# Windowed attention with two mixtures of experts: attention blocks folded on GpSimd before their transposes, the attention loop re-staggered

## The chip, the cores and the metric

The kernel runs on one core of a Trainium2 chip. The core has five engines that run their own instruction streams in order and meet through semaphores: TensorE (PE in the profile, with its weight loads as PEld), VectorE (DVE), ScalarE (ACT), GpSimd (POOL) and SyncE (SP, which here only issues DMAs). The metric is the device time of one execution in microseconds, the median of several runs.

## The reference

Three stages follow one another. Only the first is touched by the change.

```python
# q, k, v: [4 batches, 8 heads, 576 positions, 64]
scores = q @ k.T / 8 + slopes[head] * -|i - j|
scores = where(0 <= i - j < 128, scores, -1e9)        # a causal window of 128
attn = exp(scores - max(scores))
attn = attn / (sum(attn) + 1e-9)
x = (attn @ v)  -> [2304 tokens, 512]
# stage 2: soft mixture of experts
logits = x @ phi;  d = softmax over tokens;  c = softmax over slots
slots = d.T @ x;   slots = relu(slots @ w1[e]) @ w2[e];  x = c @ slots
# stage 3
out = relu(x @ w_in) ** 2 @ w_out
```

## The kernel before

**Tiling.** Heads are taken in pairs, so a unit `u` is one of 16 (batch, head pair) combinations. Its 576 queries are cut into nine chunks `c` of 64; the 64 queries of both heads fill the 128 partitions. Because of the window, a chunk sees at most three blocks of 64 keys: its own (the causal triangle), the one before (whole) and the one before that (the opposite triangle). So a score tile is 128x192, narrower for chunks 0 and 1. For a given query the triangle of the first block and that of the last one don't overlap: where one holds a weight, the other holds an exact zero.

**The attention loop.** Two consecutive chunks are one step `t`, and 72 steps cover all units. In loop iteration `t` these are written out, in this order, with manual scheduling (each engine executes its instructions in the order in which they are written):

- `emit_S(t + 1)`: two score matmuls into one of three PSUM banks "S".
- `emit_T(t - 3)`: transposes of the finished weights `p` through TensorE, into two of three PSUM banks "T": `tp` holds the blocks that fill 128 rows ("full"), `tq` those of which half is used ("half").
- `emit_PV(u)`, once in four or five steps: 24 matmuls of the transposed weights `ptb` with `v`.
- `emit_evac(t - 3, 0)`: ScalarE copies `tp` into `ptb`.
- `emit_max(t)`: VectorE adds the bias table and takes the row maximum, two instructions.
- `emit_add(t - 1)`: VectorE adds 1e-9 to the sums.
- `emit_exp(t)`: ScalarE, two exponentials with their row sums.
- `emit_norm(t - 1)`: VectorE takes reciprocals, GpSimd multiplies `p` by them, two instructions of 128x192.
- `emit_evac(t - 3, 1)`: VectorE copies the halves in `tq` into `ptb`, up to two instructions.
- `run_side(t)`: what belongs to a whole unit (`emit_xT`: ScalarE evacuates the PV result and `load_v` follows; `emit_xn`: four transposes of it and a VectorE copy), and once a batch, the logits (`emit_logits`, `emit_logr`) and the online softmax over tokens (`emit_d0` to `emit_d4`).

The loads of the next units' `z` (queries) and `k`, and one or two weight tiles of 1 MB for the second stage, are issued on SP's queue just after the score matmuls of a unit's last chunk. They land in a unit's buffers (two of each), so they wait until those score matmuls have read them. Five `p` buffers go round. `ptb` is a ring of seven groups of four 128x128 blocks; a unit takes five of them.

**After the loop** come the rest of the last batch's softmax and logits, the expert matmuls (`H`, `O`), whose weights are read while attention runs and after it, and the last stage with its 864 `acc` matmuls. Five weight tiles can only be loaded when the pools of the attention close (`load_extra`).

Of the kernel before, what the change touches and what calls it, by code (L numbers as in the profile page):

```python
# [24 lines left out]
LT = 3  # L25
# [3 lines left out]
def attn_moe_relu2_kernel(ctx: ExitStack, tc: tile.TileContext, z, k, v, phi, w1, w2, w_in, w_out, bias, cst, out):  # L29
# [22 lines left out]
    ef = const.tile([128, 32], F32, name="ef")  # L52
# [99 lines left out]
    for g in range(2 * NS):  # L152
        u, c = divmod(g, NCH)
        n = 64 * min(3, c + 1)
        e = 192 if c % 2 or (c == 0 and g % 2) else 0
        info.append((u, c, n, e))
# [11 lines left out]
    def emit_max(t):  # L168
        for i in range(2):
# [5 lines left out]
                scale=-0.125, scalar=3.0e38, op0=ALU.add, op1=ALU.min, accum_out=st_t[t][:, i:i + 1],  # L175
# [3 lines left out]
    def emit_exp(t):  # L179
        st = st_t[t]  # L180
        for i in range(2):
            u, c, n, e = info[2 * t + i]
            p = pbuf[t % NP][:, e:e + n]
            act.activation(out=p, in_=p, func=AF.Exp, bias=st[:, i:i + 1], scale=-1.0, accum_out=st[:, 2 + i:3 + i])  # L184

    def emit_add(t):
        st = st_t[t]
        dve.tensor_scalar(out=st[:, 2:4], in0=st[:, 2:4], scalar1=1e-9, scalar2=None, op0=ALU.add)  # L188

    def emit_norm(t):  # L190
        st = st_t.pop(t)
        dve.reciprocal(out=st[:, 4:6], in_=st[:, 2:4])
        for i in range(2):
            u, c, n, e = info[2 * t + i]
            p = pbuf[t % NP][:, e:e + n]
            eng = dve if t >= NS - 2 and i == 1 else pool
            eng.tensor_scalar(out=p, in0=p, scalar1=st[:, 4 + i:5 + i], scalar2=0.0, op0=ALU.mult, op1=ALU.add)  # L197

    def emit_T(t):
        full, half, P = [], [], pbuf[t % NP]
        for u, c, n, e in info[2 * t:2 * t + 2]:
            if c % 2:
                full.append((jblk(u, c // 2) + 1, e + n - 128))
                if n == 192:
                    half.append((64, jblk(u, c // 2 - 1) + 3, e))
            else:
                half.append((0, jblk(u, c // 2), e + n - 64))
                if n == 192:  # L210
                    full.append((jblk(u, c // 2 - 1) + 2, e))
        full.sort(key=lambda x: x[0])
        A = bank("T", "tp")[:, 0:256].rearrange("p (a b) -> p a b", a=2)
        B = bank("T", "tq")[:, 0:256].rearrange("p (a b) -> p a b", a=2)
        for i, (slot, e) in enumerate(full):
            pe.transpose(A[:, i, :], P[:, e:e + 128], ident)  # L216
        if len(half) == 2 and half[0][0] != half[1][0]:
            pe.transpose(B[:, 0, :], P[:, 128:256], ident)  # L218
            dst = [(ptb[r:r + 64, slot], B[r:r + 64, 0]) for r, slot, e in half]
        else:  # L220
            dst = []
            for i, (r, slot, e) in enumerate(half):
                assert r == 0 and e <= 256
                pe.transpose(B[:, i, :], P[:, e:e + 128], ident)  # L224
                dst.append((ptb[0:64, slot], B[0:64, i]))
# [150 lines left out]
    dve.memset(ptb[64:128, 0::4], 0.0)  # L376
    dve.memset(ptb[0:64, 3::4], 0.0)
# [682 lines left out]
```

## Time and profile before

| | |
|---|---|
| median of 3 runs | 402.41 us (402.33 to 402.83) |
| span of the profiled execution (first to last instruction) | 400.7 us |
| left around the span, by the median | 1.7 us |
| attention, first score matmul to the end of the last PV | 3.6 to about 130 us |
| PE / DVE / ACT / POOL busy over the span | 97 / 74 / 61 / 23 % |

The page gives busy times for the whole span, in which the last stage (from about 170 us, TensorE alone) weighs most. For the attention loop one reads stretches of it: the busy time of each engine between two points, the chain of work that ended last (followed back from the last instruction, at each step to what released it), and the rows of single forms of instructions. A PE row's duration includes the pipeline behind it, so the cost of one more matmul is read from the distance between starts, which is what the chain's pieces show.

### The profile page before, as it was taken

What the parts mean: (1) busy time and instruction counts of PE and PEld (TensorE: products, weight loads), DVE (VectorE), ACT (ScalarE), POOL (GpSimd) and SP (SyncE); (2) the same over time, 40 slices, a digit from 0 to 9 for tenths busy, and PEclk for the clock granted to TensorE, in tenths of its full rate; (3) what the DMA queues carried; (4) which work ended last, traced back from release to release, by engine and by line L of the source; (5) the groups of instructions that cost most, each with busy time, mean ns of one, the idle gap of its engine ahead of it and who ended that gap; (6) DMA issues with size and microseconds to landing.
All of it is one profiled execution on the core that took longest, in us unless ns stands there. A gap on an engine that the chain in (4) does not pass through costs nothing.

```text
span 400.7 us, 7955 instructions
## 1 busy us (share of the span) xinstructions
PE 390.5 (97%) x2666; PEld 308.0 (77%) x2666; DVE 295.5 (74%) x967; ACT 244.4 (61%) x730; POOL 90.7 (23%) x188
## 2 busy tenths in 40 slices
PE   8899999999999999999999999999999999999995
PEld 8788878878876534687787888788877888888884
DVE  6798887779877685577867789786867775566454
ACT  5788878868876411178867765777657544433440
POOL 3445435335444041213111111211010000000000
PEclk9999999999999999999999999999999999999999
DMA  7969989869896999999602200000000040013004
GB/s 234 384 231 332 369 300 361 324 236 413 308 381 228 406 421 421 407 409 408 252 2 95 90 27 0 0 2 1 0 2 2 2 157 0 2 40 117 2 0 159
DMA packets 20489, 75.36 MB, mean 188 GB/s; under 512 B 2528, under 2 KB 4320, under 8 KB 16352
## 3 DMA queue, kind: packets, MB, share of 16 engines
q1 hardware_dynamic: 19872, 74.30, 48.4%
q10 hardware_dynamic: 576, 0.56, 0.5%
q8 instruction: 21, 0.34, 0.3%
q14 instruction: 20, 0.16, 0.1%
HBM read 70.13 MB, written 4.72 MB: 187 GB/s over the span
## 4 chain that ended last, share of the span: by engine, by line
PE 89%; DVE 6%; ACT 2%; DMA 1%; issue 1%; POOL 0%; DVEq 0%; POOLq 0%
PE acc L863 48%; PE s L165 9%; PE xa L250 6%; PE h L819 4%; PE H L627 4%; PE O L766 4%; PE tp L216 3%; DVE ptb L240 2%; DVE p L173 2%; PE tq L218 1%; PE X L291 1%; PE L L278 1%; PE MX L715 1%; DVE psum L881 1%; PE tq L224 1%; PE xb L250 1%
## 5 line engine op out<-in xcount | busy, mean ns | idle before, releaser
L863 PE MATMUL acc<-whl,arena_gh 128*128 128x512 f32 x864 | 216.4, 393 | 0.0
L863 PEld LDWEIGHTS acc<-whl,arena_gh 128*128 128x128 f32 x864 | 160.2, 188 | 35.2 <-issue 2.9
L848 DVE TENSOR_TENSOR arena_gh<-hT,arena_gh 128x384 fp32r<-128x384 f32 (+1 forms) x97 | 53.7, 553 | 29.5 <-ACT arena_gh L844 24.0
L197 POOL TENSOR_SCALAR p<-p,st 128x192 f32<-128x192 f32 (+1 forms) x142 | 56.2, 408 | 68.4 <-DVE ptb L240 28.1
L184 ACT ACTIVATE p<-p,st 128x192 f32<-128x192 f32 (+1 forms) x144 | 61.3, 428 | 11.2 <-DVE st L173 10.6
L831 ACT ACTIVATE acc<-h 128x384 f32<-128x384 f32 x47 | 23.1, 491 | 64.8 <-PE h L819 64.8
L165 PE MATMUL s<-kt,zq 128*128 128x192 f32 (+2 forms) x270 | 54.3, 326 | 0.1
L675 POOL TENSOR_SCALAR yw<-f 128x512 f32<-128x512 f32 x32 | 27.2, 852 | 100.6 <-DVE arena_cin L692 49.1
L240 DVE COPY ptb<-tq 64x128 f32<-64x128 f32 x128 | 35.3, 281 | 15.2 <-PE tq L218 13.9
L173 DVE CUSTOM_DVE_ANT_0 p<-s,tbl 128x192 f32<-128x192 f32 (+1 forms) x144 | 41.7, 325 | 2.4 <-PE s L165 1.9
L165 PEld LDWEIGHTS s<-kt,zq 128*128 128x128 f32 x270 | 41.7, 195 | 1.6 <-DMA kt<-in_k_dram 0.3
L238 ACT ACTIVATE ptb<-tp 128x256 f32<-128x256 f32 (+1 forms) x72 | 25.0, 348 | 13.1 <-PE tp L216 12.5
L819 PE MATMUL h<-cst_sb,Mst 128*128 128x384 f32 x95 | 32.2, 339 | 0.1
L250 PE MATMUL xa<-ptb,vt 128*64 128x256 f32 (+1 forms) x256 | 27.8, 359 | 0.0
L184 ACT ACTIVATION_READ_ACCUMULATOR p<-p,st 128x1 f32 x144 | 27.3, 189 | 0.0
L840 DVE TENSOR_TENSOR hT<-acc 128x384 f32<-128x384 f32 x17 | 9.5, 557 | 23.6 <-ACT acc L831 23.6
L216 PE MATMUL tp<-cs,p 128*128 128x128 f32 x128 | 26.5, 276 | 0.2 <-DVE st L188 0.2
L844 ACT ACTIVATE arena_gh<-hT 128x384 fp32r<-128x384 f32 x48 | 24.8, 516 | 0.6
L844 ACT ACTIVATE arena_gh<-acc 128x384 fp32r<-128x384 f32 x47 | 24.2, 515 | 0.6
L250 PEld LDWEIGHTS xa<-ptb,vt 128*64 128x64 f32 x256 | 17.0, 136 | 9.4 <-issue 1.8
L690 DVE SCALAR_TENSOR_TENSOR yw<-f,yw 128x512 int32<-128x512 int32 x32 | 22.4, 704 | 0.8
L831 ACT ACTIVATE hT<-h 128x384 f32<-128x384 f32 x48 | 22.7, 472 | 0.0
(206 smaller groups left out, 469.1 us busy)
## 6 DMA issues: line engine op xcount, KB each, us to landing
w_w<-in_w_dram SPq DMA_DIRECT2D x31, 1024.0 KB, 8.9
f<-in_w_in_dram SPq DMA_DIRECT2D x16, 512.0 KB, 10.6
f<-in_w_out_dram SPq DMA_DIRECT2D x16, 512.0 KB, 10.2
zq<-in_z_dram SPq DMA_DIRECT2D x13, 576.0 KB, 4.7
vt<-in_v_dram SPq DMA_DIRECT2D x16, 320.0 KB, 6.7
kt<-in_k_dram SPq DMA_DIRECT2D x13, 288.0 KB, 5.3
out_dram<-psum SPq DMA_DIRECT2D x11, 256.0 KB, 2.1
yw<-in_w_dram SPq DMA_DIRECT2D x1, 1024.0 KB, 11.9
```

The source lines that it names most:

```text
L165: pe.matmul(out=sb_t[t][:, 256 * i:256 * i + n], lhsT=zbuf(u)[:, c].rearrange("p a b -> p (a b)"), rhs=kt_t[u][:, 64 * c + 64 - n:64 * c + ...
L173: dve.tensor_tensor_reduce(out=p, in0=sb_t[t][:, 256 * i:256 * i + n], in1=tbl[:, 192 * pr + 192 - n:192 * pr + 192], scale=-0.125, scalar ...
L184: act.activation(out=p, in_=p, func=AF.Exp, bias=st[:, i:i + 1], scale=-1.0, accum_out=st[:, 2 + i:3 + i])
L197: eng.tensor_scalar(out=p, in0=p, scalar1=st[:, 4 + i:5 + i], scalar2=0.0, op0=ALU.mult, op1=ALU.add)
L216: pe.transpose(A[:, i, :], P[:, e:e + 128], ident)
L240: dve.tensor_copy(out=dst, in_=src)
L250: pe.matmul(out=out, lhsT=v_t[u][:, j, po:po + 64], rhs=pt[:, a:b, po:po + 64], start=(j == 0 or (j == 3 and a == 2)), stop=(j == 4 or (j ...
L819: pe.matmul(out=hb[-1][:, 0:HB], lhsT=Mst[:, 128 * f:128 * f + 128], rhs=cst_sb[:, c0:c0 + HB], start=True, stop=True)
L831: act.activation(out=rbuf[hf][:, cl], in_=hb[hf][:, cl], func=AF.Relu)
L844: act.activation(out=lo_t[i][1][hf][:, 0, cl], in_=rbuf[hf][:, cl], func=AF.Square)
L848: eng.tensor_tensor(out=gh[hf][:, 1, cl], in0=g[hf][:, cl], in1=gh[hf][:, 0, cl].bitcast(F32), op=ALU.subtract)
L863: pe.matmul(out=acc_t[s], lhsT=gh[:, x, c0:c0 + 128], rhs=w[:, f % 2, y, :], start=(units[i] in firsts and a == 0), stop=(units[i] in last ...
```

## The change

A block of scores that is three key blocks wide was transposed as one full 128-column piece and one piece of which a half was used. Now GpSimd first subtracts the far triangle block from the near one (`emit_fold`), so that a chunk's weights stand in 128 columns, the far ones with a minus sign. One transpose per chunk is left. When the transposed block is copied out, ScalarE's Relu keeps the positive part, and VectorE takes the part with the minus sign as max(-x, 0) for the other half.

Beside it: 1e-9 is added to the row sums on GpSimd for two steps at once, and one VectorE reciprocal serves two steps (`emit_sums`, `emit_recip`); the normalising multiplication covers 128 columns in place of 192; scores are computed two steps ahead; a step's transposes come four steps after it, and their evacuation five; PV, its evacuation and the batch work move accordingly; `p` has six buffers; `ptb` has six groups of four blocks and two single ones (a unit takes four and one); the small tile `ef` lies in `phi_sb`. The first two and last two steps keep shorter distances and single sums.

```diff
-LT = 3
+LT = 4
...
-    NP = 5
+    NP = 6
...
-    NBL = 7
-    ptb = apool.tile([128, 4 * NBL, 128], F32, name="ptb")
+    NBL = 6
+    ptb = apool.tile([128, 4 * NBL + 2, 128], F32, name="ptb")
...
-    def emit_add(t):
-        st = st_t[t]
-        dve.tensor_scalar(out=st[:, 2:4], in0=st[:, 2:4], scalar1=1e-9, scalar2=None, op0=ALU.add)
+    def emit_sums(t, n=2):
+        k = 2 * (t % 2)
+        st = st_t[t // 2]
+        pool.tensor_scalar(out=st[:, 4 + k:4 + k + 2 * n], in0=st[:, 4 + k:4 + k + 2 * n], scalar1=1e-9, scalar2=1.0, op0=ALU.add, op1=ALU.mult)
+
+    def emit_recip(t, n=2):
...
+        dve.reciprocal(out=st[:, 8 + k:8 + k + 2 * n], in_=st[:, 4 + k:4 + k + 2 * n])
+
+    def emit_fold(t):
+        both = [x for x in info[2 * t:2 * t + 2] if x[2] == 192]
...
+        pool.tensor_tensor(out=ap(True), in0=ap(True), in1=ap(False), op=ALU.subtract)
 
     def emit_norm(t):
-        st = st_t.pop(t)
-        dve.reciprocal(out=st[:, 4:6], in_=st[:, 2:4])
+        st, k = st_t[t // 2], 8 + 2 * (t % 2)
+        emit_fold(t)
         for i in range(2):
             u, c, n, e = info[2 * t + i]
-            p = pbuf[t % NP][:, e:e + n]
+            o = e + n - 128 if c % 2 else e
+            p = pbuf[t % NP][:, o:o + min(n, 128)]
...
-        for dst, src in tp_t[t][i]:
-            if i == 0:
-                act.activation(out=dst, in_=src, func=AF.Copy)
+        if i == 0:
+            dst, src = tp_t[t][0]
+            act.activation(out=dst, in_=src, func=AF.Relu)
+            return
+        for dst, src, neg in tp_t.pop(t)[1]:
+            if neg:
+                dve.tensor_scalar(out=dst, in0=src, scalar1=-1.0, scalar2=0.0, op0=ALU.mult, op1=ALU.max)
             else:
                 dve.tensor_copy(out=dst, in_=src)
...
+    alone = (0, 1, NS - 2, NS - 1)
+    T_at, sums_at = {}, {}
+    for t in range(NS):
+        T_at.setdefault(t + (LT - 1 if t in alone else LT), []).append(t)
...
+    E_at = {}
+    for t in range(NS):
+        E_at.setdefault(t + (LT if t < 2 else LT + 1 if t < NS - 2 else LT - 1), []).append(t)
```

**How it moves the instructions.** On TensorE, from one PV to the next, in the middle of the attention (`s` scores, `tp`/`tq` transposes, `xa`/`xb` PV, `X` the transposes of `emit_xn`), before:

```order
L250 MATMUL xa<-ptb,vt 64x256 x6
L250 MATMUL xa<-ptb,vt 64x128 x2
L250 MATMUL xb<-ptb,vt 64x64 x4
L165 MATMUL s<-kt,zq_94 128x192 x2
L216 MATMUL tp<-cs,p_96 128x128 x2
L218 MATMUL tq<-cs,p_96 128x128
L165 MATMUL s<-kt,zq_94 128x192 x2
L216 MATMUL tp<-cs,p_97 128x128 x2
L218 MATMUL tq<-cs,p_97 128x128
```

and now:

```order
L261 MATMUL xa<-ptb,vt 64x256 x6
L261 MATMUL xa<-ptb,vt 64x128 x2
L261 MATMUL xb<-ptb,vt 64x64 x4
L166 MATMUL s<-kt,zq_93 128x192
L166 MATMUL s<-kt,zq_92 128x64
L233 MATMUL tp<-cs,p_99 128x128 x2
L166 MATMUL s<-kt,zq_92 128x128
L166 MATMUL s<-kt,zq_92 128x192
L233 MATMUL tp<-cs,p_100 128x128 x2
```

A step's third transpose (`tq`) is gone and everything else of a step stands; over the program the transposes into the "T" banks of this loop are 144 in place of 208 (128 into `tp`, 80 into `tq`).

On GpSimd, two steps before (each line is one head pair's chunk):

```order
L197 TENSOR_SCALAR p_97<-p_97,st 128x192 [waits DVE_49,PE_49,Activation_49]
L197 TENSOR_SCALAR p_97<-p_97,st 128x192 [waits Activation_49]
L197 TENSOR_SCALAR p_98<-p_98,st 128x192 [waits DVE_49,PE_49,Activation_49]
L197 TENSOR_SCALAR p_98<-p_98,st 128x192 [waits Activation_49]
```

and two steps now, the sums first, then fold, norm, norm for either step:

```order
L190 TENSOR_SCALAR st<-st 128x4 [waits Activation_49]
L209 TENSOR_TENSOR p_95<-p_95 128x2x64 [waits PE_49]
L219 TENSOR_SCALAR p_95<-p_95,st 128x128 [waits DVE_49,Pool_49]
L219 TENSOR_SCALAR p_95<-p_95,st 128x128
L209 TENSOR_TENSOR p_96<-p_96 128x2x64 [waits PE_49]
L219 TENSOR_SCALAR p_96<-p_96,st 128x128 [waits Pool_49]
L219 TENSOR_SCALAR p_96<-p_96,st 128x128
```

Four instructions became seven; the first of them waits for ScalarE's exponentials of the later step, and VectorE's reciprocal waits for it.

On TensorE at the end of the loop, before (from the last score matmuls on):

```order
L165 MATMUL s<-kt,zq_93 128x192 x2
L216 MATMUL tp<-cs,p_98 128x128
L224 MATMUL tq<-cs,p_98 128x128 x2
L216 MATMUL tp<-cs,p_99 128x128 x2
L224 MATMUL tq<-cs,p_99 128x128
L250 MATMUL xa<-ptb,vt 64x256 x6
```

and now:

```order
L166 MATMUL s<-kt,zq_92 128x192 x2
L233 MATMUL tp<-cs,p_100 128x128 x2
L233 MATMUL tp<-cs,p_95 128x128 x2
L233 MATMUL tp<-cs,p_96 128x128 x2
L302 MATMUL X<-cs,xT_103 128x128 x4
L306 MATMUL Y<-cs,xT_103 128x128
L233 MATMUL tp<-cs,p_97 128x128 x2
L233 MATMUL tp<-cs,p_98 128x128 x2
L233 MATMUL tp<-cs,p_99 128x128 x2
L261 MATMUL xa<-ptb,vt 64x256 x6
```

The scores of the last step come before more of the remaining transposes, and the last PV but one comes later. The last batch's first logits (`L`), which stood ahead of the last PV, now stand behind it.

## Rows read from the trace of the kernel before

**Rows 1.** Busy time by stretch: us, engine busy (x instructions), clock, DMA share, GB/s.

```profile
15.70:122.00 106.30, 104.73 (x989) 87.70 (x989) 88.16 (x507) 85.12 (x359) 48.23 (x123) 1.00 0.87 331
122.00:128.46 6.46, 5.74 (x71) 3.90 (x68) 5.43 (x26) 4.08 (x17) 3.45 (x8) 1.00 0.62 226
```

**Rows 2.** Chain of waits, 15.7 to 122 us, its shares by line.

```profile
by line: PE s L165 29.5%; PE xa L250 21.9%; PE tp L216 9.1%; DVE ptb L240 6.0%; PE X L291 4.5%; DVE p L173 4.3%; PE tq L218 4.1%; PE tq L224 3.4%; PE xb L250 3.0%; PE R L336 2.9%; PE L L278 2.9%; issue 1.5%; DVE st L192 1.3%; PE L L284 1.2%
```

**Rows 3.** Chain of waits, 15.7 to 43 us: start us, us, what.

```profile
15.75 1.66 PE xa L250 x16
...
18.82 0.65 PE s L165 x4
19.47 0.22 PE tp L216 x2
19.69 0.11 PE tq L218
...
29.30 1.67 PE xa L250 x16
```

**Rows 4.** Chain of waits, 43 to 62 us, where it leaves TensorE.

```profile
47.51 0.29 DVE ptb L240
...
47.82 0.28 DVE ptb L240
48.10 0.27 DVE p L173
...
48.66 0.09 DVE st L188
...
48.77 0.17 DVE st L192
...
48.97 0.29 DVE ptb L240
```

**Rows 5.** Groups by form, 22 to 118 us: count, busy us, mean ns, idle before.

```profile
L184 ACT ACTIVATE p<-p,st 128x192 f32<-128x192 f32 x87 | 38.7, 446 | 7.7 <-DVE st L173 7.3
L240 DVE COPY ptb<-tq 64x128 f32<-64x128 f32 x99 | 27.4, 281 | 11.4 <-PE tq L218 10.5
L238 ACT ACTIVATE ptb<-tp 128x256 f32<-128x256 f32 x42 | 15.7, 373 | 6.5 <-PE tp L216 6.0
L296 DVE COPY xn_all<-X 128x512 f32<-128x512 f32 x13 | 8.9, 683 | 0.2
L262 ACT ACTIVATE xT<-xa 128x512 f32<-128x512 f32 x13 | 7.5, 581 | 1.1 <-PE xa L250 1.1
```

**Rows 6.** GpSimd's groups by form, whole span.

```profile
L197 POOL TENSOR_SCALAR p<-p,st 128x128 f32<-128x128 f32 x16 | 6.0, 372 | 5.6 <-DVE st L192 2.1 <-PE s L165 1.4 <-ACT p L184 1.4
L197 POOL TENSOR_SCALAR p<-p,st 128x64 f32<-128x64 f32 x16 | 5.1, 317 | 14.8 <-PE s L165 5.5 <-ACT p L184 5.1 <-DVE st L192 4.2
L707 POOL TENSOR_TENSOR whl<-arena_co,whl 128x512 fp32r<-128x512 f32 x2 | 2.6, 1278 | 10.6 <-ACT whl L706 10.6
L935 POOL COPY stat<-arena_gh 128x1 f32<-128x1 f32 x1 | 0.2, 183 | 8.8 <-DVE arena_gh L848 8.8
```

**Rows 7.** Instructions in order of time, end of the attention loop.

```profile
123.33 1.74 PE L250 MATMUL xa<-ptb,vt 128*64 128x256 f32 x16
...
124.58 0.34 DVE L173 CUSTOM_DVE_ANT_0 p<-s,tbl 128x192 f32<-128x192 f32 x1
...
126.86 0.86 PE L278 MATMUL L<-xT,phi_sb 128*32 128x128 f32 x24
...
128.46 1.74 PE L250 MATMUL xa<-ptb,vt 128*64 128x256 f32 x16
...
130.24 0.60 ACT L262 ACTIVATE xT<-xa 128x512 f32<-128x512 f32 x1 [1.33 <-PE xa L250]
```

**Rows 8.** Loads of `k`: from issue to landing.

```profile
DMA to landing us min/median/max: 2.8/5.2/7.5
```

More of the change, by code (lines that the diff above doesn't have):

```diff
@@ L154, in attn_moe_relu2_kernel @@
         n = 64 * min(3, c + 1)
-        e = 192 if c % 2 or (c == 0 and g % 2) else 0
+        e = 192 + 192 - n if c % 2 else 192 if c == 0 and g % 2 else 0
         info.append((u, c, n, e))
@@ new lines, in emit_recip, with ap @@
+    def emit_recip(t, n=2):
+        k = 2 * (t % 2)
+        st = st_t[t // 2]
+        dve.reciprocal(out=st[:, 8 + k:8 + k + 2 * n], in_=st[:, 4 + k:4 + k + 2 * n])
+    def emit_fold(t):
+        both = [x for x in info[2 * t:2 * t + 2] if x[2] == 192]
+        both.sort(key=lambda x: x[3])
+        if not both:
+            return
+        def ap(near):
+            o = [e + (0 if near == (c % 2 == 0) else 128) for u, c, n, e in both]
+            x = pbuf[t % NP][:, o[0]:o[0] + 64]
+            l = [list(y) for y in x.ap]
+            return bass.AP(tensor=x.tensor, offset=x.offset, ap=[l[0], [o[-1] - o[0], 2], [1, 64]]) if len(o) == 2 else x
+        pool.tensor_tensor(out=ap(True), in0=ap(True), in1=ap(False), op=ALU.subtract)
@@ L201, in emit_T @@
     def emit_T(t):
-        full, half, P = [], [], pbuf[t % NP]
+        full, rest, P = [], [], pbuf[t % NP]
         for u, c, n, e in info[2 * t:2 * t + 2]:
[L204 to L207, printed above, removed]
-            else:
-                half.append((0, jblk(u, c // 2), e + n - 64))
-                if n == 192:
-                    full.append((jblk(u, c // 2 - 1) + 2, e))
+            if c == 0:
+                rest.append((e, 0, jblk(u, 0), False))
+            elif c % 2:
+                full.append((jblk(u, c // 2) + 1, e + n - 128, (64, jblk(u, c // 2 - 1) + 3, True) if c > 1 else None))
+            else:
+                full.append((jblk(u, c // 2 - 1) + 2, e, (0, jblk(u, c // 2), True)))
@@ L212, in emit_T @@
         full.sort(key=lambda x: x[0])
         A = bank("T", "tp")[:, 0:256].rearrange("p (a b) -> p a b", a=2)
[L214 to L225, printed above, removed]
+        for i, o in enumerate([x[1] for x in full] + [x[0] for x in rest]):
+            pe.transpose(A[:, i, :], P[:, o:o + 128], ident)
@@ L226, in emit_T @@
         sl = [x[0] for x in full]
         st = sl[1] - sl[0] if len(sl) == 2 else 1
-        if st < 0:
-            raise AssertionError
-        tp_t[t] = [(ptb[:, sl[0]:sl[-1] + 1:st], A[:, 0:len(sl)])], dst
+        half = [(i, *x[2]) for i, x in enumerate(full) if x[2]] + [(len(full) + i, *x[1:]) for i, x in enumerate(rest)]
+        tp_t[t] = (ptb[:, sl[0]:sl[-1] + 1:st], A[:, 0:len(sl)]), [(ptb[r:r + 64, slot], A[r:r + 64, i], neg) for i, r, slot, neg in half]
     def jblk(u, j):
-        return 4 * ((5 * u + j) % NBL)
+        return 4 * ((4 * u + j) % NBL) if j < 4 else 4 * NBL + u % 2
```

63 lines of the change are left out of this document (37 added, 26 removed).

## The prediction

> **What bounds the kernel now.** I read three views of the attention loop, which ends near 130 us; the change touches nothing behind it. First the busy times of its even part, 15.7 to 122 us: TensorE is busy for 104.7 of 106.3 us, VectorE and ScalarE for 83 and 80%, GpSimd for 45% [rows 1]. A busy TensorE may be a pipeline that is only long, so the chain of waits comes second. Its shares by line add up to some 83% on TensorE (scores 29.5%, PV 25%, `tp` and `tq` 16.6%) and to 12% on VectorE [rows 2]. Third, the chain piece by piece, which has two patterns. From 15.75 to 29.30 us, two units, it never leaves TensorE (but for 0.02 us): four score matmuls in 0.65 us, two `tp` in 0.22, one `tq` in 0.11, and the next scores start at once [rows 3]. Elsewhere it runs through VectorE step after step: two half copies of 0.29 and 0.28, two maxima of 0.27, the addition 0.09, the reciprocal 0.17, and 1.46 us after the first copy the next step's copy [rows 4].
>
> So two engines are nearly level. Two units cost TensorE 13.55 us where it never waits [rows 3]. Between the PV at 15.75 and the one at 123.33 lie 14 units [rows 3, 7], 15.37 us a pair. The batch work on the chain (lines 278, 284, 336: 7.0% of 106.3 us, 7.4 us [rows 1, 2]) is 1.06 a pair. TensorE thus needs 14.6 of 15.37 us, and what it waits is at most 0.76 a pair, 5.3 us in all. VectorE has nine steps of 1.46, less two halves that a pair of units lacks (0.56), and two `xn` copies of 0.683 [rows 4, 5]: 13.9 us before batch work, the same as TensorE.
>
> One rule of the Trainium skill (Perfetto Trace Analysis, Identifying the Most-Contended Engine) says to judge TensorE's headroom by the share of its weight loads, not of its matmuls. That row says 87.7 of 106.3 us, 82% [rows 1], a level with VectorE. By that rule TensorE would have a sixth of its time free here; it is a rival below. A chain that stays on TensorE through two whole units speaks against it.
>
> **What the change takes from TensorE.** 144 transposes are left of 208. Each stands in the chain with 0.11 us [rows 3], in stretches without a wait as in the others: 64 x 0.11 = 7.0 us, eight per pair of units, and 13.55 becomes 12.67. Nothing else of a step's TensorE work changes. If another engine set the pace everywhere, this would be worth nothing; 7.0 is the upper end unless waits go too.
>
> **VectorE.** The addition goes (0.09 and 0.02 to its next), and every second reciprocal (0.17 and 0.03) [rows 4]: 9 x 0.11 + 4.5 x 0.20 = 1.9 us a pair, 13.9 becomes 12.0. The 112 halves that are now max(-x, 0) read the same 64x128 from PSUM as the copies, 281 ns [rows 5]; I take them at that price. Off the path, a tenth more would cost 112 x 0.03 = 3.4 us of an engine that has 12% room.
>
> **ScalarE.** The count stays; Relu replaces Copy in 72 evacuations at 373 ns [rows 5]. Nine steps of two exponentials (446 ns) and one evacuation are 11.4 us, two `xT` 1.2 [rows 5]: 12.5 us a pair, an upper figure because neighbours overlap.
>
> **GpSimd.** This is where the work goes. Its normalisations shrink: a 128x128 one takes 372 ns, a 128x64 one 317 [rows 6]; 16 and two a pair are 6.6 us. The fold is not in the trace of before. It reads two blocks and writes one, at most 128 columns, so it is bounded below by the 128x128 row with one input (372 ns) and above by the only two-input row, 1278 ns for 512 columns [rows 6]. The 64 and 128 rows give a fixed part of 262 ns and 0.86 ns a column; with that fixed part the 512 row gives 1.98 ns a column for two inputs, so an estimate of 0.52 us for two blocks and 0.39 for one. It is nearer to the upper row in kind and to the lower one in size, and I take 0.52. A pair of units has six of the one and two of the other: 3.9 us. The sums lie between the 183 ns of one column and the 317 of 64 [rows 6]; 4.5 x 0.25 = 1.1. GpSimd then needs 11.6 us a pair, after 7.0 now (45% of 15.37 [rows 1]).
>
> With batch work TensorE needs 12.67 + 1.06 = 13.7 us a pair; the other three 11.6 to 12.5 before theirs. TensorE stays first, by about a tenth, so its saving is not handed to another engine at once.
>
> **The new wait.** A reciprocal now waits for GpSimd's sums, they wait for both steps' exponentials, and they are queued behind the multiplications of the two steps before. Behind the reciprocal on VectorE stand that step's halves and the next maxima, and ScalarE waits for those. What hides it: scores lie two steps ahead in place of one, transposes come a step later, and two transposes need one "T" bank where three needed two, so TensorE may run a step further from the others. Before, a `tq` waited for the previous evacuation, and 11.4 us of VectorE's idle time before its copies are waits for `tq` [rows 5]. I can't price cover gained against latency added. So I leave TensorE's waits as they are: 0, with bounds of -3 (more than half of the 5.3 go) and +4 (they nearly double).
>
> **The ends.** At the start scores and loads come in the same pieces; 0, within 0.5 either way. At the end, before, the last maximum ends at 124.92 and the last PV starts at 128.46 [rows 7]. Now nine halves stand behind VectorE's last multiplication in place of six, 3 x 0.28 = 0.8 us; the last transposes no longer stand behind 1.1 us of logits (126.86 to 127.98); those logits follow the PV, where 0.6 us of `xT` hides half of them [rows 7]. Together between -0.6 and +1.4, and I take +0.5. What follows attention moves with it: the late weight tiles are issued when attention's pools close.
>
> **DMA.** 331 GB/s at a share of 0.87 [rows 1] are 35.2 MB, or 92 us at a full share. The stretch becomes about 99.5 us, so the loads fit, without much room. `k` lands 5.2 us after issue, 7.5 at worst [rows 8]; it is due about five steps later, 7.0 us at TensorE's own pace (5 x 12.67 / 9).
>
> **Sum.** 400.7 - 7.0 + 0.5 = 394.2 us of span; with the 1.7 us around it 395.9 against the median of 402.4.
>
> **The rivals.**
> - *The waits go as well.* With a bank to spare and scores further ahead the chain never leaves TensorE, as in [rows 3]: another 3 us, 392.9. For it: the first 28 us have no wait already, and VectorE loses 1.9 us a pair. Against: the batch stretches give every engine a burst that no buffer covers.
> - *The hand-over to GpSimd stretches the steps.* Sums, fold and four multiplications are one queue of about 2.6 us for two steps, as long as two steps on the other engines; TensorE then waits for `p`. With waits nearly doubled (+4): 399.9.
> - *TensorE isn't the bound*, by the weight-load rule. Then only the VectorE part of the chain shrinks: 12% of 106.3 us, by 0.21 of 1.46, 1.8 us, and with +0.5 at the end 401.1.
> - *Loads come late.* After a double weight load `k` lands at 7.5 us and is due at about 6.4 (five steps less a score group): 1.1 us in each of the four such units, 400.3.
> - *Slower: GpSimd becomes the pace.* If a fold costs what the 512 row costs, a pair is 8 x 1.278 + 6.6 + 1.1 = 17.9 us against 15.37, eight pairs 20 us more, near 422. It decides from a fold of (15.37 - 7.7) / 8 = 0.96 us. The Trainium skill (GPSIMD Engine Reference, Engine selection) says to keep two-input elementwise work on VectorE, because GpSimd takes about twice as long, 2.6 cycles an element; from its figure a fold would be an estimated 0.28 us and a fixed part, which is not the 0.96. No row of this trace has a two-input operation of this width.
>
> That the transposes don't go is excluded by the order of the instructions.
>
> **Chances.** Forecast (393.9 to 398.2): 0.50. Waits go too: 0.18. Stretched steps: 0.15. TensorE not the bound: 0.07. Late loads: 0.04. GpSimd the pace: 0.06. A difference under 0.2% (0.8 us) could not be told from none here; 0.02 of the share of "TensorE isn't the bound" lies there, and 0.01 of the stretched steps. So faster 0.91, same 0.03, slower 0.06. For 8 in 10 the range runs from 392.6, which takes in most of the waits' rival, to 400.2, which takes in most of the stretched steps.
>
> **What would show it.** Right: the PV-to-PV distance of a quiet pair falls from 13.55 to about 12.7; the chain's transposes are 0.22 a step; a fold's row stands near 0.5 us and GpSimd is busy 75 to 85% in the loop; the chain behind attention is as long as before. Wrong: a chain that runs through GpSimd's multiplications or waits of VectorE's reciprocal for GpSimd; folds over 0.9 us; score matmuls that wait for `k`.

## The result, and the profile after

The changed kernel takes **405.49 us** (median of 13 runs, 403.54 to 408.38) against 402.41 (13 runs, 402.21 to 404.02): ratio 1.0072, 95% interval 1.0057 to 1.0087. It is slower, where 395.9 was forecast. Its runs scatter, with a mean granted clock of 0.985 to 0.996 over the span; the profiled execution of before had 0.998. That mean also counts the stretch behind the last matmul, where the rows show 0.50: 1.7 us before, which is all of its 0.002, and 3.9 us in the changed kernel's profile, so a mean of 0.996 need not be a fall of the clock during the work. The profiled execution took 407.58 us with a span of 405.7. Runs over 1.5% above the fastest of their kernel (two of e6_efirst, one each of e11_dead and e12_warm) are in the medians below but not in the ratios; without them these medians are 403.76, 407.27 and 399.06.

Busy times by stretch, the columns as in [rows 1]: the loop, then what follows the last scores.

```profile
15.70:118.00 102.30, 97.69 (x926) 80.37 (x925) 77.53 (x415) 83.37 (x358) 71.62 (x209) 1.00 0.90 341
118.00:130.00 12.00, 7.75 (x46) 5.11 (x45) 6.09 (x27) 5.43 (x22) 5.76 (x16) 0.72 0.39 133
```

VectorE fell from 83 to 76% and ScalarE stands at 81%; GpSimd rose from 45 to 70%, somewhat less than the 75 to 85% that the prediction named. But TensorE went from 98.5 to 95.5%, and the second row is new: 65% busy, at a granted clock of 0.72. The chain of waits from 15.7 to 118 us, by line, has 16% of transfers; [rows 2] lists none:

```profile
by line: PE s L166 25.9%; PE xa L261 18.0%; DMA vt<-in_v_dram 10.3%; PE tp L233 8.5%; DMA kt<-in_k_dram 6.1%; DVE xn_all L307 3.8%; DVE p L174 3.5%; PE X L302 3.3%; PE L L289 3.0%; PE R L347 2.9%; PE xb L261 2.5%; DVE ptb L249 2.3%; issue 1
```

Piece by piece, a step without a wait is just as forecast: 0.65 us of scores and 0.22 of transposes, 0.87 in place of 0.98 [rows 3].

```profile
15.29 0.65 PE s L166 x4
15.95 0.22 PE tp L233 x2
...
29.07 0.61 DVE xn_all L307
29.68 0.21 DVE p L174
...
30.17 0.92 PE s L166 x4
```

The last three pieces are new: a copy of `xn`, then the maxima behind it, and only then scores. The groups by form, 22 to 118 us, answer [rows 5, 6]: fold, halves, Relu, sums and reciprocal.

```profile
L209 POOL TENSOR_TENSOR p<-p 128x128 f32<-128x128 f32 x38 | 17.4, 458 | 1.5
L249 DVE TENSOR_SCALAR ptb<-tp 64x128 f32<-64x128 f32 x88 | 25.0, 284 | 13.3 <-ACT ptb L245 11.8
L245 ACT ACTIVATE ptb<-tp 128x256 f32<-128x256 f32 x44 | 16.3, 370 | 2.9 <-PE tp L233 2.6 <-ACT xT L278 0.2
L190 POOL TENSOR_SCALAR st<-st 128x4 f32<-128x4 f32 x28 | 5.4, 194 | 16.3 <-ACT p L185 15.4
L195 DVE RECIPROCAL st<-st 128x4 f32<-128x4 f32 x28 | 4.9, 175 | 3.4 <-POOL st L190 3.0
```

No price was at fault: the fold is 0.46 us (0.52 estimated), the sums 0.19 (0.25), halves and Relu cost what the copies did. The new wait for GpSimd costs VectorE 3.0 us in 28 reciprocals. What went wrong stands among TensorE's instructions in order of time (in brackets: idle time before and what ended it):

```profile
14.39 0.68 PE L166 MATMUL s<-first 128*128 128x64 f32 x4 [1.42 <-DMA first<-in_k_dram]
68.80 1.74 PE L261 MATMUL xa<-ptb,vt 128*64 128x256 f32 x16 [1.70 <-DMA vt<-in_v_dram]
92.61 0.92 PE L166 MATMUL s<-kt,zq 128*128 128x192 f32 x4 [0.55 <-DVE st L174]
122.65 1.09 PE L233 MATMUL tp<-cs,p 128*128 128x128 f32 x4 [2.40 <-POOL st L190]
124.23 0.66 PE L233 MATMUL tp<-cs,p 128*128 128x128 f32 x2 [0.49 <-DVE ptb L251]
124.82 3.26 PE L261 MATMUL xa<-ptb,vt 128*64 128x256 f32 x16
```

The last line is PV(14) of 16; every other PV takes 1.74 us, as in [rows 7]. Where the 11.5 us between the forecast span (394.2) and this one lie, by milestones (starts of first matmuls; in the new order three score groups and two transposes more, 2.17 us, stand ahead of each PV but the last):

| stretch, us | before | forecast | after | missed by |
|---|---|---|---|---|
| start to PV(0) | 15.68 | 15.68 + 2.17 - 5 x 0.11 = 17.30 | 17.95 | 0.65 |
| loop, PV(0) to PV(13) | 100.29 | less 51 x 0.11: 94.7 | 97.72 | 3.0 |
| end, PV(13) to the expert matmuls `H` | 21.95 | less 2.17 and 8 x 0.11, plus 0.5: 19.4 | 24.95 | 5.55 |
| `H` to the first `acc` | 35.18 | same | 35.86 | 0.7 |
| `acc` to the end | 227.55 | same | 229.24 | 1.7 |

The last two rows say little about the change. `O` waits once for a weight tile (0.48 us), as in one profile below (0.46 in e8_sums_dve) and in no other; and from VectorE's last instruction to the end of the span it is 5.3 us here, 3.0 to 4.1 in the other profiles. Together they are about what separates this execution from the median. So two stretches need a cause: the loop (3.0 us) and the end (5.5 us).

For the loop, PV(0) to PV(13), the busy times of before and after (columns as above) split the 3.0:

```profile
15.68:115.97 100.29, 98.72 (x936) 82.28 (x935) 83.49 (x477) 80.11 (x339) 45.87 (x117) 1.00 0.86 326
17.95:115.67 97.72, 93.11 (x884) 76.61 (x884) 73.48 (x391) 79.14 (x338) 68.13 (x199) 1.00 0.90 337
```

TensorE's busy time fell by 5.6 us, 51 transposes of 0.11; its idle time rose from 1.6 to 4.6. Of that, 2.1 us are six waits of scores for the maxima, 1.7 one wait for `v`, 0.4 one for `k`.

### The profile page after: what moved, and what is told of

It reads as the page before. It is cut to its first block, busy times and chain, and to the rows that moved or that the text cites. A ratio compares the mean times of both kernels' runs of the same rounds, so it can differ in the third digit from the quotient of the medians.

```text
span 405.7 us, 7885 instructions
## 1 busy us (share of the span) xinstructions
PE 386.2 (95%) x2602; PEld 302.2 (74%) x2602; DVE 282.5 (70%) x862; ACT 243.7 (60%) x730; POOL 118.3 (29%) x291
## 4 chain that ended last, share of the span: by engine, by line
PE 79%; DMA 10%; DVE 5%; ACT 2%; issue 1%; SPq 1%; POOL 1%; ACTq 0%; DVEq 0%
PE acc L890 48%; PE s L166 7%; PE xa L261 6%; PE h L846 4%; PE H L654 4%; DMA w_w<-in_w_dram 3%; DMA kt<-in_k_dram 3%; DMA vt<-in_v_dram 3%; PE tp L233 3%; DMA first<-in_k_dram 2%; DVE xn_all L307 1%; PE L L289 1%; PE MX L742 1%; DVE psum L908 1%; DVE p L174 1%; PE X L302 1%
## 5 line engine op out<-in xcount | busy, mean ns | idle before, releaser
L185 ACT ACTIVATE p<-p,st 128x192 f32<-128x192 f32 (+1 forms) x144 | 61.3, 428 | 14.1 <-DVE st L174 11.4
L166 PE MATMUL s<-kt,zq 128*128 128x192 f32 (+2 forms) x270 | 55.2, 329 | 3.2 <-DVE st L174 2.7
L219 POOL TENSOR_SCALAR p<-p,st 128x128 f32<-128x128 f32 (+1 forms) x142 | 50.6, 371 | 13.7 <-DVE ptb L251 5.7
L249 DVE TENSOR_SCALAR ptb<-tp 64x128 f32<-64x128 f32 x112 | 31.9, 284 | 20.5 <-ACT ptb L245 18.6
L261 PE MATMUL xa<-ptb,vt 128*64 128x256 f32 (+1 forms) x256 | 29.3, 373 | 2.7 <-DMA vt<-in_v_dram 1.7
L245 ACT ACTIVATE ptb<-tp 128x256 f32<-128x256 f32 (+1 forms) x72 | 25.0, 348 | 11.5 <-PE tp L233 8.7
L233 PE MATMUL tp<-cs,p 128*128 128x128 f32 x144 | 28.1, 282 | 3.2 <-POOL st L190 2.4
L209 POOL TENSOR_TENSOR p<-p 128x128 f32<-128x128 f32 (+1 forms) x64 | 27.1, 424 | 2.7
L233 PEld LDWEIGHTS tp<-cs,p 128*128 128x128 f32 x144 | 19.6, 148 | 5.5 <-POOL st L190 2.6
```

The costliest lines, as they stand in the source:

```text
L166: pe.matmul(out=sb_t[t][:, 256 * i:256 * i + n], lhsT=zbuf(u)[:, c].rearrange("p a b -> p (a b)"), rhs=kt_t[u][:, 64 * c + 64 - n:64 * c + ...
L185: act.activation(out=p, in_=p, func=AF.Exp, bias=st[:, k + i:k + i + 1], scale=-1.0, accum_out=st[:, 4 + k + i:5 + k + i])
L209: pool.tensor_tensor(out=ap(True), in0=ap(True), in1=ap(False), op=ALU.subtract)
L219: eng.tensor_scalar(out=p, in0=p, scalar1=st[:, k + i:k + i + 1], scalar2=0.0, op0=ALU.mult, op1=ALU.add)
L233: pe.transpose(A[:, i, :], P[:, o:o + 128], ident)
L249: dve.tensor_scalar(out=dst, in0=src, scalar1=-1.0, scalar2=0.0, op0=ALU.mult, op1=ALU.max)
```

## The experiments

Times are medians; the ratio is to the kernel before in runs taken beside each kernel, with its 95% interval. Loop and end are the stretches of the table above, from each one's profile.

| kernel | loop | end | us | ratio |
|---|---|---|---|---|
| before | 100.29 | 21.95 | 402.4 to 402.8 | |
| changed | 97.72 | 24.95 | 405.49 | 1.0072 (1.0057 to 1.0087) |
| e1_tail | 97.31 | 20.40 | 401.10 | 0.9967 (0.9938 to 0.9997) |
| e2_v_early | 96.76 | 24.47 | 405.21 | 1.0059 (1.0023 to 1.0094) |
| e3_both | 96.66 | 20.37 | 400.74 | 0.9975 (0.9936 to 1.0014) |
| e4_fold_old | 101.07 | 21.68 | 404.35 | 1.0050 (1.0020 to 1.0080) |
| e5_warm | 100.23 | 23.58 | 404.06 | 1.0036 (1.0009 to 1.0062) |
| e6_efirst | 98.41 | 23.45 | 403.99 | 1.0001 (0.9964 to 1.0038) |
| e7_s4t2 | 103.73 | 24.59 | 411.06 | 1.0207 (1.0152 to 1.0262) |
| e8_sums_dve | 97.53 | 24.23 | 406.55 | 1.0094 (1.0055 to 1.0133) |
| e9_s4t2_both | 104.56 | 21.21 | 408.70 | 1.0145 (1.0101 to 1.0188) |
| e10_xn | 96.14 | 20.38 | 400.57 | 0.9930 (0.9897 to 0.9964) |
| e11_dead | 99.78 | 22.91 | 407.31 | 1.0123 (1.0058 to 1.0188) |
| e12_warm | 95.45 | 20.37 | 399.18 | 0.9909 (0.9884 to 0.9934) |

### The end of the loop: e1_tail, e6_efirst, e5_warm

VectorE of the changed kernel behind the last maxima:

```profile
121.18 0.17 DVE L195 RECIPROCAL st<-st 128x2 f32<-128x2 f32 x1 [0.70 <-POOL st L190]
121.72 0.28 DVE L219 TENSOR_SCALAR p<-p,st 128x128 f32<-128x128 f32 x1 [0.37 <-POOL p L209]
121.92 0.58 DVE L249 TENSOR_SCALAR ptb<-tp 64x128 f32<-64x128 f32 x2
```

The half copies, which free a T bank, stand behind a reciprocal and a multiplication, and both wait for GpSimd. They end at 122.50; TensorE's transposes start at 122.65. (The list above puts that wait down to GpSimd's sums, the event nearest in time; the bank is what the transposes write to, and e6_efirst tests it.) PV(14) is queued behind those transposes and two more, though all it needs was transposed by 119.1.

```diff
 # e1_tail: PV(14) ahead of the transposes of step 68, what follows it and the copies of steps 67 to 69 a step earlier
+        t0 = (NCH * u + 8) // 2 + (LT + 1 if u < NU - 2 else LT if u == NU - 2 else LT - 1)
...
+        if t == NS:
+            emit_PV(NU - 2)
         for x in T_at.get(t, ()):
...
 # and (this alone is e6_efirst) the half copies ahead of the reciprocal, from iteration 71 on
+        if t >= NS - 1:
+            for x in E_at.get(t, ()):
+                emit_evac(x, 1)
         if done[1]:
             emit_recip(*done)
```

> The changed kernel with its last iterations in another order: PV(14) stands on TensorE ahead of the transposes of step 68 (before: behind those of step 70), the copies of steps 67 to 69 come one step earlier, and from iteration 71 on VectorE makes the half copies ahead of the reciprocal. Theory 'tail' (the loss lies behind the last scores: in the changed kernel VectorE's half copies stand behind a reciprocal and a multiplication that wait for GpSimd, so TensorE waits 2.4 us for a T bank with PV(14) queued behind, and then works at the 1.2 GHz level for some 6 us, PV(14) 3.26 us in place of 1.74): PV(14) takes 1.74, the last PV starts near 125.5 to 126.5 in place of 130.04, the second stage 9.5 us behind it in place of 10.6, the time falls by 4 to 5 from 405.5 to about 401, and runs agree within 1 us again. Theory 'loads' (the transfers bound the first 170 us, so that time gained at the end of attention comes back as waits for weights in the second stage): the last PV comes earlier, but the wait of O for its last weight tile grows by the same, and the time stays at 404 or more. Theory 'hand-over' (the steps of the loop are stretched by the new wait for GpSimd): nothing changes in the loop, at most 1 us.

Measured: 401.10, 4.4 us less than the changed kernel, the end 24.95 to 20.40. PV(14) starts at 120.20, the last PV at 126.64, `H` 9.45 us behind it, and the clock stays at 1.00:

```profile
120.20 1.83 PE L261 MATMUL xa<-ptb,vt 128*64 128x256 f32 x16
...
125.14 0.44 PE L233 MATMUL tp<-cs,p 128*128 128x128 f32 x2 [1.12 <-POOL p L219]
125.51 0.86 PE L289 MATMUL L<-xT,phi_sb 128*32 128x128 f32 x24
```

The last line is a third part of this edit: with PV(14) the logits behind it move up too and stand ahead of the last PV again, as before. In the changed kernel the last PV waits 1.02 us for ScalarE's copy of PV(14) and the logits follow it. `O` waited for no weights, so the theory that transfers take the gain back later falls. Runs still scatter (399.4 to 404.7): that part of the expectation missed, see e5_warm.

> The changed kernel where from iteration 71 on VectorE makes the half copies ahead of the reciprocal and the multiplication; PV(14) and all else stay in their places. It splits the tail's 4.4 us. If the wait for the T bank is what counts (VectorE's copies behind the reciprocal that waits for GpSimd): TensorE's gap of 2.4 us shrinks to 1.5 or less, the clock stays at 1.00, and 2 to 3 us come back: 402.5 to 403.5. If PV(14)'s place behind the transposes of step 70 is what counts: the gap moves to these transposes, which wait for p, and the time stays above 404.5.

Measured: 403.99, 1.5 us back, between the two. The gap shrank to 0.90 us, but another of 1.21 followed at the transposes of step 70, and then the clock fell all the same (columns as above):

```profile
122.00 0.85 PE L233 MATMUL tp<-cs,p 128*128 128x128 f32 x4 [0.90 <-POOL st L190]
124.06 0.54 PE L233 MATMUL tp<-cs,p 128*128 128x128 f32 x2 [1.21 <-DVE st L195]
```
```profile
124.00:125.00 1.00, 0.94 (x4) 0.50 (x6) 0.48 (x2) 0.00 (x0) 0.84 (x2) 0.60 0.25 106
```

The split of the 4.4 us is not settled by this. Three of the runs, with a mean clock of 0.998 or more, took 400.5 to 401.8, close to e1_tail; the other seven took 403.7 to 410.4, and the ratio of 1.0001 has an interval 3 us wide. In the profile the end is 3.05 us longer than in e1_tail; in it lie 1.13 us more behind the last PV, where the logits stand, a wait of 1.02 before it, and some 3 us at a clock of 0.50. How much PV(14)'s place is worth by itself stays open.

```diff
 # e5_warm: the changed kernel
         for x in T_at.get(t, ()):
+            if x == NS - 4:
+                keep_warm("S", 20, idle)
```

> The changed kernel with 20 matmuls of 128x128 without a use on TensorE ahead of the transposes of step 68, where it waited 2.4 us for a T bank (20 x 0.11 = 2.2 us, so they fit the gap). Nothing else moves. Theory 'clock' (the part of the tail's loss that is the 1.2 GHz level behind the idle gap): the granted clock stays at 1.00 from 118 to 131 us, PV(14) takes 1.74 us in place of 3.26, the last PV starts near 128 in place of 130.04, the time falls by about 2 from 405.5 to 403.5, and the scatter of the runs (403.5 to 408.4) shrinks. Theory 'order' (the wait for the T bank and PV(14) behind the transposes is all): within 0.5 of 405.5, and the scatter stays.

Measured: 404.06. The filler was twice as long as meant (the trace has each of its matmuls as two of 0.11 us, 4.5 us in all against a gap of 2.4), and still the kernel gained 1.4 us. PV(14) takes 1.74 us, and the clock in the end stays at 1.00. The changed kernel there, then this one:

```profile
122.00:128.00 6.00, 4.86 (x26) 3.06 (x28) 3.28 (x13) 1.04 (x3) 2.28 (x6) 0.50 0.23 90
```
```profile
122.00:128.00 6.00, 5.62 (x50) 5.41 (x51) 3.37 (x15) 2.48 (x12) 4.42 (x12) 1.00 0.56 215
```

The clock is thus a part of the end's loss by itself: at 0.50 from 122 to 128 us, PV(14) alone 1.52 us longer. The scatter did not go: six runs with a mean clock of 0.998 or more took 402.8 to 404.4, four with 0.996 took 405.3 to 406.6. The profile, one of the four, shows one reason. Its longest wait for `v`, at PV(7), was 2.23 us, and behind it the clock fell in the middle of the loop:

```profile
69.73 2.68 PE L261 MATMUL xa<-ptb,vt 128*64 128x256 f32 x16 [2.23 <-DMA vt<-in_v_dram]
```
```profile
70.00:72.00 2.00, 2.00 (x16) 1.25 (x14) 0.40 (x4) 0.00 (x0) 1.20 (x4) 0.59 0.98 409
```

### The loads of v: e2_v_early, e3_both

SyncE's issues in the changed kernel, in order of time. PV(5) had freed the buffer by 55.7, but the load of `v` is written with `emit_xT`, which now comes an iteration later, behind the loads for later units; it is issued behind two weight tiles of 1 MB and lands 10.5 us later:

```profile
56.84 0.43 SPq L142 DMA_DIRECT2D kt<-in_k_dram  x1
57.31 0.90 SPq L70 DMA_DIRECT2D w_w<-in_w_dram  x2
58.26 0.53 SPq L146 DMA_DIRECT2D vt<-in_v_dram  x1
```

```diff
 # e2_v_early
         for a in side0.get(t, ()):
             emit_PV(*a)
+        for a in side0.get(t, ()):
+            if a[0] + NQ < NU:
+                load_v(a[0] + NQ)
...
-            if f is emit_xT and a[0] + NQ < NU:
-                load_v(a[0] + NQ)
```

> The changed kernel with the load of v issued in the iteration of its PV, so that it stands ahead of the next z, k and weight tiles on SyncE's queue, as in the kernel before (changed: one iteration later, behind them). Theory 'loads, by their order': the 1.70 us wait of PV(7) for v goes and v lands within 6 us; 403.8 (405.5 - 1.7). Theory 'loads, by their sum' (the queue is full): the wait moves to k or to weights, 405.5. Theories 'tail' and 'hand-over': the waits of the scores for VectorE's maxima (2.1 us) and the end stay as they are; at most the 1.7.

Measured: 405.21; `v` is issued at 55.05, no PV waits for it, and the loop is 0.96 us shorter. Not 1.7, because the next unit's scores then wait:

```profile
70.68 0.68 PE L166 MATMUL s<-kt,zq 128*128 128x64 f32 x4 [1.19 <-DVE ptb L249]
```

The list names VectorE's copies, the nearest event, but these scores read `kt`, issued at 63.49 and landed 7.0 us later, at 70.5. So most of the wait moved from `v` to `k`, as the theory of the sum has it; the six waits for the maxima stay at 2.1 us. The end stays (24.47), with a mean clock of 0.983 to 0.994 in every run, and the 0.96 does not show in the median beyond the scatter.

> Both edits, the order of the last iterations and the early load of v. If the losses are two independent ones: 405.5 - 4.5 - 1.7 = 399.3. If the transfers as a whole bound the first 170 us: no better than the better one of the two alone, and O waits over 2 us for weights. If the hand-over stretched the steps: 404 or more.

Measured: 400.74, which e1_tail's 401.10 can't be told from (the loop is 0.65 us shorter). Five of six runs lie within 400.2 to 401.0, the sixth at 404.93; e10_xn below has both edits too and scatters from 398.2 to 402.9, so the late `v` and the gap at the end are not all of the scatter. Scores now wait 3.8 us for VectorE, 1.4 of them ahead of PV(0), and 0.7 for `k`; weights in `O` don't bind.

### Fold and distances apart: e4_fold_old, e11_dead

```diff
 # e4_fold_old: the fold alone; emit_sums on VectorE, one step at a time
-LT = 4
+LT = 3
-        for x in (1, 2) if t == 0 else (t + 2,) if t + 2 < NS else ():
+        for x in (t + 1,) if t + 1 < NS else ():
...
 # e11_dead: the changed kernel, in 64 steps
+            pe.transpose(D[:, 0, :], P[:, full[0][1]:full[0][1] + 128], ident)
```

> The fold alone on the old distances: one transpose per chunk, GpSimd folds, but scores one step ahead, transposes and copies three steps after the scores' step, the addition and the reciprocal on VectorE for every step as in the kernel before, five p buffers, PV, v and batch work where they were. If the order (the longer tail and the late v) spoiled the gain of the fold: 64 x 0.11 = 7.0 us of TensorE fall away and the end is as long as before: 396 to 398. If VectorE and GpSimd set the pace on the old distances (VectorE's 13.9 us a pair stay, and a fold of 0.46 us comes into the way of p): 401 to 404, with chains through VectorE's copies and GpSimd's multiplications in every step. If the transfers bound: 400, with waits for k and v.

Measured: 404.35, and the loop is 0.8 us longer than before although TensorE has 51 transposes less in it. The chain leaves TensorE for the way of one step through ScalarE and GpSimd (first lines); and of TensorE's 6.0 us of idle time in the loop 3.7 are three waits of the batch work for VectorE's `dn`, which no other kernel here has (last lines: total, times, longest):

```profile
20.13 0.95 ACT p L185 x4
...
21.09 0.38 POOL p L219
```
```profile
PE R L347 <- DVE dn L340: 2.5, 2, 1.2
PE R L347 <- DVE dn L342: 1.2, 1, 1.2
PE tp L233 <- ACT p L185: 1.0, 3, 0.5
```

On the old distances `p` and the batch's softmax aren't ready in time, and the fold gives nothing there. That is the second case of the expectation in kind, though by line the chain is more ScalarE's (15% in its exponentials) than VectorE's copies (4%).

> The changed kernel with a third transpose of 0.11 us in 64 steps, into a free part of the same bank, which nobody reads: TensorE does as much as in the kernel before, all else is as in the changed one. Theory 'TensorE is the pace of the loop between the waits': 52 x 0.11 = 5.7 us more up to PV(13), less what the late loads give back (they come no later; up to 2.1 us), so PV(13) at 119.3 to 121.4 in place of 115.67, and about 409 to 412. Theory 'the loop is paced by the other engines or by the transfers': the waits shrink by as much as the transposes cost, PV(13) within 2 us of 115.67, and at most 407.5.

Measured: 407.31, PV(13) at 118.23, the loop 99.78: between the two cases, 2.06 us more for 5.6 us of transposes. Most of the other 3.5 came out of the waits. Who waited for whom on TensorE, 15 to 118 us (us in total, times, longest), in the changed kernel and in this one:

```profile
PE s L166 <- DVE st L174: 2.1, 6, 0.5
PE xa L261 <- DMA vt<-in_v_dram: 1.7, 1, 1.7
PE s L166 <- DMA kt<-in_k_dram: 0.4, 1, 0.4
```
```profile
PE s L166 <- DVE st L174: 0.9, 5, 0.3
PE s L166 <- DMA kt<-in_k_dram: 0.3, 1, 0.3
PE xa L264 <- DMA vt<-in_v_dram: 0.2, 1, 0.2
```

So the loop takes 100.3 us before, 101.1 with the fold on the old distances, 99.8 with the whole change but as many transposes as before, and 97.7 with the whole change. The new distances are what makes the fold worth something, and of the 5.6 us that it takes from TensorE 3.5 are lost to waits that the transposes would have covered. (New distances without GpSimd's fold were not run, and e4_fold_old also has the sums on VectorE, so this is no clean two by two.)

### The hand-over to GpSimd: e8_sums_dve

```diff
-        pool.tensor_scalar(out=st[:, 4 + k:4 + k + 2 * n], in0=st[:, 4 + k:4 + k + 2 * n], scalar1=1e-9, scalar2=1.0, op0=ALU.add, op1=ALU.mult)
+        dve.tensor_scalar(out=st[:, 4 + k:4 + k + 2 * n], in0=st[:, 4 + k:4 + k + 2 * n], scalar1=1e-9, scalar2=None, op0=ALU.add)
```

> The changed kernel with the addition of 1e-9 for two steps on VectorE in place of GpSimd, so that the reciprocal no longer waits for GpSimd's queue; everything else stays. Theory 'hand-over' (the wait for GpSimd holds VectorE up, and with it the maxima and the scores): the waits of the scores for VectorE (2.1 us) halve, and at the end the reciprocals no longer wait 0.7 us; 402 to 403.5. Theories 'tail' and 'loads': VectorE pays 36 x 0.1 us more and nothing on the path changes but the 0.7 us at the end; 404.5 to 406.

Measured: 406.55, the loop 97.53 against 97.72, scores wait 2.1 us for VectorE as in the changed kernel. The hand-over as a cause falls: VectorE's 3.0 us of waiting for the sums were not on the path. The median is higher, but the interval overlaps that of the changed kernel; the runs have a mean clock of 0.981 to 0.996.

### Score banks and VectorE's order: e7_s4t2, e9_s4t2_both, e10_xn, e12_warm

```diff
 # e7_s4t2; e9_s4t2_both: the same on e3_both
-    NBUF = {"S": 3, "T": 3, "xa": 1, "B": 1}
+    NBUF = {"S": 4, "T": 2, "xa": 1, "B": 1}
```

> The changed kernel with four score banks and two T banks in place of three and three. Theory 'score banks' (with scores two steps ahead, the third score bank is free only when the maximum of the step before is done, so each batch of xn copies on VectorE, 0.69 us, comes straight onto TensorE): the six waits of the scores for VectorE, 2.1 us, go; 403.4 (405.5 - 2.1) if the T banks suffice. Rival 'T banks' (a step's transposes are copied a step later, so two banks are both held): new waits of tp for the copies of the same size or more, 405 to 410.

> Four score banks and two T banks together with the other order of the last iterations and the early load of v. If the three losses (tail, v behind the weight tiles, score banks) are separate: e3_both's 400.7 less 2.1 to 3.8 (the waits of the scores for VectorE there): 397 to 398.6. If two T banks are too few: 402 or more.

Measured: 411.06 and 408.70, the rival in both. A block that is copied a step later holds its T bank a step longer; in e7_s4t2 transposes and the batch work that shares these banks wait some 11 us. Four score banks beside three T banks were not tried, so whether they would help by themselves stays open.

```diff
 # e10_xn: e3_both, and the xn copy behind the next maximum
+        late_xn.append(lambda: dve.tensor_copy(out=xn_all[:, :, sl], in_=X.rearrange("p (g d) -> p g d", g=4)))
-        dve.tensor_copy(out=xn_all[:, :, sl], in_=X.rearrange("p (g d) -> p g d", g=4))
...
             emit_max(t)
+        while late_xn:
+            late_xn.pop(0)()
```

> The kernel with both edits (order of the last iterations, early load of v), and VectorE's copy of xn now stands behind the next step's maximum instead of ahead of it. Theory 'VectorE's order' (with scores two steps ahead a score bank is only free when the maximum of the step before is done, and the xn copy of 0.69 us stands right ahead of that maximum; it also waits for the transposes X, while the maximum could already be taken): the waits of the scores for VectorE, 3.8 us with both edits and 2.1 in the changed kernel, fall under 1 us; about 398.5 (400.7 - 2.1), better than both kernels. Rival 'VectorE's work' (the copy delays the half copies and the reciprocal by as much): the waits move to tp, and the time stays within 0.7 of 400.7.

Measured: 400.57 (11 runs, 398.2 to 402.9), ratio 0.9930; the loop is 0.5 us shorter than in e3_both. The median is the rival's, 2 us above the theory's, and the interval overlaps that of e3_both. But the kernel is faster than the one before, every wait of scores for the maxima is gone, and `tp` waits only 0.5 us. What is late next is the load of `k` (the first line is ahead of PV(0); a third wait, 1.16 us at 69.89, is that of e2_v_early again, `k` issued at 62.68 and landed 7.1 us later):

```profile
PE s L166 <- DMA first<-in_k_dram: 2.2, 1, 2.2
PE s L166 <- DMA kt<-in_k_dram: 1.5, 2, 1.4
```

And its first two units show what a quiet pair was forecast to do:

```profile
18.52 1.66 PE xa L261 x16
...
31.20 0.80 PE xa L261 x6
```

12.68 us from 18.52 to 31.20, in place of 13.55 [rows 3]. By line the chain of that stretch holds nothing but TensorE:

```profile
by line: PE s L166 47.6%; PE xa L261 26.2%; PE tp L233 16.4%; PE X L302 6.9%; PE xb L261 3.6%
```

```diff
 # e12_warm: e10_xn, and
+            if x == NS - 1:
+                keep_warm("S", 4, idle)
```

> The last kernel (other order of the last iterations, early v, xn copy behind the maximum) with four matmuls of 128x128 without a use ahead of the last step's transposes, where TensorE waited 1.12 us for p (each is two passes of 0.11 us, 0.9 us in all, so they fit). Its runs lay between 398.2 and 402.9 us, the longer ones with a mean granted clock of 0.993 to 0.996 in place of 0.998 to 1.000. Theory 'clock behind the gaps of the tail': with the gap filled all runs keep a clock of 0.998 or more and lie between 398 and 400.5, median about 399. Rival 'the clock falls elsewhere, or for another reason': the same scatter, median 400 to 401.

Measured: **399.18**, ratio 0.9909 (0.9884 to 0.9934), the best here and faster than both kernels. Five of six runs lie between 398.4 and 400.2 with a clock of 0.998 or more, the sixth at 404.45 with 0.992. That fits the gap at the end as a source of the scatter, but not as the only one, and it isn't shown: the interval overlaps that of e10_xn, the end of the two profiles is the same (20.37 and 20.38) though the gap shrank from 1.12 to 0.22, and the long run was not profiled.

## Why the prediction was wrong

- **The transposes' 7.0 us: right as a price, wrong as a saving.** A step costs 0.87 us as forecast, and the quiet pair came out at 12.68 where 12.67 was worked out. TensorE's busy time in the loop fell by the 5.6 us that 51 transposes are; the loop by 2.6. I had called 7.0 the upper end and then used it.
- **TensorE's waits, taken at 0 with bounds of -3 and +4: they grew by 3.0, the first step that failed, though inside its bounds.** I read up to 5.3 us of waits in the kernel before from a difference of means; between PV(0) and PV(13) its TensorE is idle for 1.6, so there was next to nothing to win. The changed kernel's is idle for 4.6. Where the chain runs through VectorE [rows 4] TensorE was not idling; the two engines were level, and shortening one of two level engines makes it wait for the other. 2.1 us of the waits are the maxima behind the `xn` copy (e10_xn), 1.7 the late `v` (e2_v_early). Beside it a reading: of VectorE's 11.4 us of idle time before its copies, [rows 5] puts 10.5 down to `tq`, not all.
- **Loads come late: a rival that came true in part, at 0.04, with the wrong tile.** I priced `k` after a double weight load at 1.1 us. In the changed kernel `k` cost 0.4 us in the loop, and `v` 1.7, because moving `emit_xT` moved its load past the next weight tiles on SyncE's queue. I had followed the moved step's own instruction and not the DMA that it issues (e2_v_early). With `v` early the price of `k` comes out: 1.19 us in e2_v_early, 0.74 in e3_both, 1.41 in e12_warm, at the same scores. The start, 0 within 0.5, took 0.65 us more; TensorE waits there before the third unit's first scores in both kernels (1.45 and 1.42 us, now for `k`), and what the rest is stays open.
- **The ends, +0.5 with bounds of -0.6 and +1.4: measured +6.05 (5.55 over the forecast), the term mis-sized most, and outside its bounds.** I counted instructions behind the last multiplication. I did not ask what TensorE does in between: the last score matmul starts at 118.16 and the last transposes at 128.43, 10.3 us later; before it was 121.84 and 127.99, 6.2 us. A longer distance is cover in the loop and an empty queue at its end. In it, PV(14) stood behind transposes that waited, the granted clock fell, and the logits behind the last PV were on the path with all of their 1.1 us rather than half: from the last PV's start to `H` 10.58 us in place of 9.46. Another order of these iterations gave back 4.4 us of the time, 4.55 of the end (e1_tail); how it splits over the three is not shown.
- **GpSimd the pace, and the stretched hand-over: rightly held unlikely or wrongly feared.** The fold is 0.46 us, far under the 0.96 from which it would decide, and e8_sums_dve shows that the hand-over costs the loop nothing (97.53 against 97.72). At the same 128x128, two inputs cost 458 ns and one 376, a factor of 1.2. The Trainium skill (GPSIMD Engine Reference, Engine selection) says about twice as long as on VectorE, which is another comparison; no run here has this fold on VectorE.
- **TensorE isn't the bound, by the weight-load rule:** weight loads fill 79% of the loop (80.37 of 102.30), so by the Trainium skill (Perfetto Trace Analysis, Identifying the Most-Contended Engine) a fifth would be free. The traces agree in part: of 5.6 us put back, 2.06 showed (e11_dead), yet a pair without late work runs on TensorE from end to end (e10_xn).

What stays open: the scatter that is left, how the end's loss splits, and what earlier loads of `k` would give, which was not tried.

## What to carry to other kernels

When one engine is only a little ahead of the others, work taken from it buys the distance to the next one and no more; read that distance from idle time in the stretch, not from a chain's shares or from means. A longer software pipeline has to be paid at its end: write the last iterations in an order of their own, with independent work ahead of what waits. And when a step moves, follow the DMAs that it issues through the queue that they are issued on.

## What the hardware showed

The granted clock fell to the lower of its two levels (1.2 of 2.4 GHz; 0.50 in the rows) in or behind idle gaps of TensorE of 2.40 us (the changed kernel), 2.23 (e5_warm), and of 0.90 and 1.21 close together (e6_efirst). It stayed there for 3 to 7 us, also while TensorE worked again without a break, and nearly doubled the time of a PV (1.74 to 3.26). It did not fall behind 2.21 us at the start of e10_xn, behind 2.14 in e11_dead, nor behind 1.12 in e1_tail:

```profile
14.90:18.50 3.60, 3.60 (x26) 3.28 (x27) 2.64 (x19) 2.67 (x12) 3.05 (x10) 1.00 1.06 411
```

So gaps of nearly the same length went either way. Where the clock falls, a short wait can cost about as much again as it lasts (in the changed kernel, an estimate: 4.86 busy us at 0.50 from 122 to 128 us are 2.4 more than at 1.00, behind a gap of 2.40), and that it does not always fall would show as scatter. The Trainium skill (TensorE: Matmul & The Clock Gate, HAM oscillation — how this bites in real kernels) describes such falls for waits for transfers; the late `v` in e5_warm is one, and at the end of the loop the clock fell without one.
